# Experts' lists with entries of 64 B, written whole, in a kernel of decayed attention and a mixture of experts

## The chip, the core and the metric

The kernel runs on one core of a Trainium2 chip. The core has five engines with instruction streams of their own: TensorE (PE in the profile; its weight loads stand apart as PEld), VectorE (DVE), ScalarE (ACT), GpSimd (POOL) and SyncE (SP), which here only issues transfers. All transfers run on 16 DMA engines that the queues share: SP's and ACT's own queues, and a software queue that POOL issues on and that serves the indirect transfers, which scatter or gather rows by a list of indices. The metric is the device time of one execution in microseconds.

## The reference

```python
# attention with decay, per batch and head: 8 x 8 x 576 x 64
scores = (q @ k.T) / sqrt(64)
ret = scores * Dmat            # gamma_h ** (i - j) for i >= j, else 0
attn = ret @ v
# the rows of all heads side by side: x is 4608 x 512
logits = x @ w_gate            # 512 x 8
e_idx = argmax(logits, axis=1) # one expert of 8 for each token
gate_w = softmax(logits)[e_idx]
eom = sigmoid(x @ w_output_gate)
for e in range(8):
    mask = e_idx == e
    out[mask] = gate_w * eom[:, e] * (relu(x[mask] @ w1[e]) @ w2[e])
```

w1 is 8 x 512 x 1024, w2 is 8 x 1024 x 512; everything is float32. The scale of a row, `gate_w * eom`, is worked out as one reciprocal.

## The kernel before

**Retention part.** The 4608 tokens are 36 tiles of 128 rows, and a loop over `g` does one tile a step. SP loads the tile's q, k and v (`pk`, 768 KB in two transfers, five buffers, issued five steps ahead behind products of PE). POOL scales q (`prep_q`, `qs`, two steps ahead) and v (`prep_v`, `vs`, one step ahead). PE forms score products (`scores`), the result (`out_x`) and the running state (`update`), and transposes k (`k_rows`); DVE masks the scores and transposes the result, SP stores it to `xs` in DRAM (256 KB a step); ACT copies it to `xT` (line 413).

**Gate.** For each group of four tiles (`n`, nine groups) PE forms the logits, and the steps `gate_a`, `ranks`, `gate_b`, `exp_a`, `exp_b`, `gate_d` and `gate_c` give for each token its expert, its slot in that expert's list and its scale. The list `lst` lies in DRAM: eight lists of 4608 entries. An entry is two words, the token's number and its scale. `meta` holds both in SBUF, a pair of words for each of the 36 tiles; the numbers come from `tokid` by one load, `gate_c` writes the scales. Each tile's 128 entries go to `lst` by one indirect transfer of POOL (`scatter`, line 517, behind a memset of `tick`), queued in `todo` and issued one to two a step by `some`. Before the first scatter, `fill` writes all of `lst` with empty entries (token 4608, scale 0).

**Lists.** The main pass takes at most 616 tokens of an expert, as two parts of 360 and 256. `load_idx` reads the slots of these parts from `lst` to `lists` in SBUF on SP's queue, every 32 of them copied to all four quarters of the partitions, and `make_idx` turns them into indices on DVE: `idx` for whole rows, `gidx` for quarters of rows. This happens first for experts 0 and 1, part 0, behind step 30 (line 278, `make_idx` at step 32), and once more for everything else behind the last group's scatters. Each `load_idx` waits for every scatter so far. The rows themselves are gathered from `xs` by POOL (`gather_rows`, `gather`).

**Experts.** Each expert's products (`mm1`, `mm2`) split a float32 operand in a high and a low part and sum three products. The first three blocks of expert 0 run while the last group's gate is still being worked out; `transp_pe` of its part 1 (line 223, `t_ps`) is where PE needs the second list load. Tokens past 616 of an expert would be done by a loop at the end whose number of trips is read from `ovn`, a table that `overflow_table` makes at expert 1.

The order on each engine is the order in which the code is written; a scheduler doesn't move it.

Of the kernel before, what the change touches and what calls it, by code (L numbers as in the profile page):

```python
# [24 lines left out]
E = 8  # L25
# [17 lines left out]
SLOT = [[2 * (2 * (k % 2) + (c - k // 2) % 2) + k // 2 for c in range(2)] for k in range(4)]  # L43
NOV = 40


@with_exitstack
def tile_retention_moe(
# [28 lines left out]
    xs = dram.tile([NT + 1, DM], F32, name="xs")  # L77
    lst = dram.tile([E * NT, 2], I32, name="lst")

# [27 lines left out]
    def load_rest(step):  # L107
        if step == 1:
            SP.dma_start(out=wg_sb, in_=wg)
            SP.dma_start(out=csm_sb, in_=csm)  # L110
        if step == 2:
            SP.dma_start(out=cbf_sb, in_=cbf)
            SP.dma_start(out=meta, in_=tokid)

# [9 lines left out]

    NZ = E * NT // P // 3
    zw = xta.tile([P, KB * NW[0]], F32, name="xh0")[:, 0:512]
    zl = hpa.tile([P, NW[0]], I32, name="hh00")[:, 0:2 * NZ].rearrange("p (r w) -> p r w", w=2)
# [124 lines left out]
    def mm2(e, t, between={}):  # L252
# [3 lines left out]
        for fb in range(FB):  # L256
            wh, wl = (a[:, fb % 2, :] for a in W2[e, fb // 2])
            hh, hl = HT[e, part, fb]
            for a, b in ((hh, wh), (hh, wl), (hl, wh)):
                i = T.matmul(ps, lhsT=a[:, c0:c0 + n], rhs=b, start=(j == 0), stop=(j == 3 * FB - 1))  # L260
                j += 1
                if j in between:
# [4 lines left out]
                             in_=y, in_offset=None, bounds_check=NT - 1, oob_is_err=False)  # L267

    def load_idx(e0, e1, part):
        s0, t0, nb = part * NS[0], part * 4 * TA, NB[part]  # L270
        rest = NS[part] - 32 * nb
        view = lst.rearrange("(e a s) w -> e a s w", e=E, a=1)
        dmas = []
        if e1 - e0 < 4:

            for e in range(e0, e1):
                v = view[e, :, s0:s0 + 32 * nb].rearrange("a (j t) w -> a j (t w)", t=nb).broadcast_to([4, 32, 2 * nb])
                dmas.append(SP.dma_start(out=lists[:, e, t0:t0 + nb].rearrange("p t w -> p (t w)"), in_=v))
# [12 lines left out]
    def make_idx(e0, e1, part):  # L291
        n, t0 = (TA, 0) if part == 0 else (CT - TA, TA)
        V.tensor_scalar(out=gidx[:, e0:e1, 4 * t0:4 * (t0 + n)], in0=lists[:, e0:e1, 4 * t0:4 * (t0 + n), 0],
                        scalar1=4.0, scalar2=quad, op0=ALU.mult, op1=ALU.add)
        for a in range(4):
            q = slice(32 * a, 32 * a + 32)
            V.tensor_copy(idx[q, e0:e1, t0:t0 + n],
                          lists[q, e0:e1].rearrange("j e (t u) w -> j e t u w", u=4)[:, :, t0:t0 + n, a])

# [207 lines left out]
    def gate_c(n):  # L507
        zs, sli = gt["zs"], gt["sli"]
        es = sm.tile([P, GT, 1], F32, name="es")
        V.tensor_reduce(out=es, in_=gt["ex"], op=ALU.add, axis=AX.X)  # L510
        V.tensor_scalar(out=zs, in0=zs, scalar1=1.0, scalar2=None, op0=ALU.add)
        V.scalar_tensor_tensor(out=zs, in0=es, scalar=1e-9, in1=zs, op0=ALU.add, op1=ALU.mult)
        V.reciprocal(out=meta.bitcast(F32)[:, n * GT:(n + 1) * GT, 1:2], in_=zs)  # L513

        def scatter(t, dep=None):
            G.memset(tick, 0.0)
            i = G.indirect_dma_start(out=lst, out_offset=bass.IndirectOffsetOnAxis(ap=sli[:, t, :], axis=0),  # L517
                                     in_=meta[:, n * GT + t, :], in_offset=None)
# [19 lines left out]
    V.memset(zl[:, :, 0:1], NT)  # L538
    V.memset(lists, 0)
    V.memset(lists[:, :, :, 0:1], NT)  # L540
    factors(1)
# [7 lines left out]
    for g in range(NTILE):  # L549
# [183 lines left out]
    with ExitStack() as octx:  # L733
# [43 lines left out]
def _consts():  # L777
# [20 lines left out]
    tok = np.arange(NT).reshape(NG, GT, 4, 32).transpose(1, 3, 0, 2).reshape(P, NTILE)  # L798
    tok = np.stack([tok, 0 * tok], axis=2)
    f = np.float32  # L800
# [47 lines left out]
```

## Time and profile before

| | |
|---|---|
| runs | 609.34 us median of 3 (606.75 to 609.36) |
| profiled execution | 610.28 us, of which the span of its instructions 608.5 us |
| mean granted clock of TensorE | 0.984 |
| busy, share of the span: PE, PEld, DVE, ACT, POOL | 577.9 us 95%, 511.3 us 84%, 328.9 us 54%, 170.0 us 28%, 317.0 us 52% |
| DMA | 93.30 MB, 153 GB/s on the mean; 40.6% of the engines' time for SP's queue, 10.4% for POOL's |
| scatters to `lst` | 36, from 40.3 us to 179.0 us |

A row of a view gives a line of the code, the engine, the operation, what it writes and reads, how often, and its time; what stands in square brackets or behind the last bar is the time that the engine was idle before it, and what ended that. "issue" is a wait that the profile cannot name. In the rows of slices, each place is a stretch of time and each digit the busy share in tenths; a busy share of PE takes in time in which a product is waiting in the pipeline.

### The profile page before, as it was taken

The numbers are of one execution on the slowest core, as the hardware profiler recorded it, in microseconds if no ns is written. First come the engines' busy times: TensorE is split into PE (matmuls) and PEld (weight loads), VectorE is DVE, ScalarE is ACT, GpSimd is POOL, SyncE is SP. The second block draws the span as 40 slices with busy tenths as digits, with TensorE's granted clock in tenths as the row PEclk, the third lists the DMA queues.
The fourth block names the chain that finished last, engine by engine and source line by source line (L and its number), as shares of the span: only waits on it lengthen the run. The fifth ranks groups of instructions, "written<-read, shape, count | busy, mean of one in ns | idle before, by whom it ended". The sixth has DMA issues, their size and how long they took to land. (4 is left out here: it accounts for less than half of the span.)

```text
span 608.5 us, 14048 instructions
## 1 busy us (share of the span) xinstructions
PE 577.9 (95%) x5737; PEld 511.3 (84%) x5737; DVE 328.9 (54%) x640; ACT 170.0 (28%) x360; POOL 317.0 (52%) x333
## 2 busy tenths in 40 slices
PE   7989798888899999999999999999999999999995
PEld 4878687777797989979988997998899799879974
DVE  3567577576772769735841862484187239426300
ACT  5434233223542322132222221222222222212210
POOL 4778588675766754464453545345345534540011
PEclk9999899888999999999999999999999999999999
DMA  8899999877965546422721552263155216321001
GB/s 325 270 321 245 201 253 260 229 215 191 248 152 123 169 162 196 143 74 88 233 95 50 180 172 71 78 209 107 65 157 165 97 48 225 118 67 52 1 36 44
DMA packets 52420, 93.30 MB, mean 153 GB/s; under 512 B 10878, under 2 KB 30335, under 8 KB 52354
## 3 DMA queue, kind: packets, MB, share of 16 engines
q1 hardware_dynamic: 42690, 71.87, 40.6%
q0 software_dynamic: 9232, 19.93, 10.4%
q8 instruction: 46, 0.75, 0.5%
q10 hardware_dynamic: 432, 0.59, 0.3%
q14 instruction: 20, 0.16, 0.1%
HBM read 73.19 MB, written 19.86 MB: 153 GB/s over the span
## 5 line engine op out<-in xcount | busy, mean ns | idle before, releaser
L180 POOL DMA_INDIRECT x_q<-xs,gidx x140 | 148.0, 1057 | 108.6 <-ACT hh L248 71.0
L244 PE MATMUL h_ps<-xh,w1l 128*128 128x360 f32 (+1 forms) x512 | 154.6, 302 | 0.0
L244 PE MATMUL h_ps<-xh,w1h 128*128 128x360 f32 (+1 forms) x512 | 154.6, 302 | 0.0
L244 PE MATMUL h_ps<-xl,w1h 128*128 128x360 f32 (+1 forms) x512 | 154.5, 302 | 0.0
L260 PE MATMUL y_ps<-w2h,hh 128*128 128x512 f32 (+1 forms) x320 | 125.1, 391 | 0.3 <-ACT hh L248 0.3
L260 PE MATMUL y_ps<-w2l,hh 128*128 128x512 f32 (+1 forms) x320 | 124.8, 390 | 0.0
L260 PE MATMUL y_ps<-w2h,hl 128*128 128x512 f32 (+1 forms) x320 | 124.7, 390 | 0.0
L266 POOL DMA_INDIRECT out_dram<-y,idx x40 | 40.8, 1020 | 120.8 <-ACT y L265 105.7
L244 PEld LDWEIGHTS h_ps<-xh,w1l 128*128 128x128 f32 x512 | 96.9, 189 | 0.2 <-issue 0.2
L244 PEld LDWEIGHTS h_ps<-xl,w1h 128*128 128x128 f32 x512 | 96.2, 188 | 0.5
L244 PEld LDWEIGHTS h_ps<-xh,w1h 128*128 128x128 f32 x512 | 96.1, 188 | 0.5 <-issue 0.2
L248 ACT ACTIVATE hh<-h_ps 128x360 fp32r<-128x360 f32 (+1 forms) x128 | 54.6, 429 | 144.8 <-PE h_ps L244 143.8
L249 DVE SCALAR_TENSOR_TENSOR hl<-h_ps,hh 128x360 fp32r<-128x360 f32 (+1 forms) x128 | 58.5, 473 | 67.7 <-ACT hh L248 67.6
L260 PEld LDWEIGHTS y_ps<-w2h,hl 128*128 128x128 f32 (+1 forms) x320 | 58.8, 184 | 14.4 <-DVE hl L249 0.4
L260 PEld LDWEIGHTS y_ps<-w2h,hh 128*128 128x128 f32 (+1 forms) x320 | 58.8, 184 | 14.2 <-ACT hh L248 0.7
L260 PEld LDWEIGHTS y_ps<-w2l,hh 128*128 128x128 f32 (+1 forms) x320 | 58.7, 184 | 13.5
L265 ACT ACTIVATE y<-y_ps,idx 128x512 f32<-128x512 f32 (+1 forms) x40 | 27.5, 688 | 130.1 <-issue 68.9
L374 DVE TENSOR_TENSOR S_sb<-sc,cmat_sb 128x512 f32<-128x512 f32 x72 | 46.1, 681 | 29.6 <-PE sc L370 29.4
L336 POOL TENSOR_TENSOR qs<-pk,gq_sb 128x512 f32<-128x512 f32 x36 | 46.0, 1277 | 23.8 <-DMA pk<-in_pack_dram 9.0
L217 DVE TENSOR_TENSOR xl<-x_t,xh 128x512 fp32r<-128x512 f32 (+1 forms) x35 | 23.5, 673 | 64.0 <-ACT xh L214 64.0
L370 PEld LDWEIGHTS sc<-qs,pk 64*64 64x64 f32 x1152 | 28.6, 138 | 20.5 <-issue 14.2
L517 POOL DMA_INDIRECT lst<-meta,sli x36 | 37.6, 1043 | 14.2 <-DVE meta L513 9.0
(120 smaller groups left out, 623.5 us busy)
## 6 DMA issues: line engine op xcount, KB each, us to landing
st<-in_w_dram SPq DMA_DIRECT2D x61, 512.0 KB
pk<-in_pack_dram SPq DMA_DIRECT2D x31, 512.0 KB
pk<-in_pack_dram SPq DMA_DIRECT2D x32, 256.0 KB
xs<-xq SPq DMA_DIRECT2D x40, 128.0 KB
pk<-in_pack_dram SPq DMA_DIRECT2D x4, 768.0 KB
x_q<-xs,gidx POOLq DMA_INDIRECT x140, 3.9
xs<-w2h SPq DMA_DIRECT2D x16, 128.0 KB
xs<-w2l SPq DMA_DIRECT2D x16, 128.0 KB
```

The lines of the kernel that those rows point to most:

```text
L180: after(G.indirect_dma_start(out=XG[e, t][:, u, :], out_offset=None, in_=xs.rearrange("t (a c) -> (t a) c", a=4), in_offset=bass.IndirectO ...
L217: V.tensor_tensor(out=lo, in0=src[:, :, 0:n], in1=hi.bitcast(F32), op=ALU.subtract)
L244: T.matmul(ps, lhsT=a[:, k, :], rhs=b[:, k, :], start=(j == 0), stop=(j == 3 * KB - 1))
L248: done = A.activation(out=hh, in_=ps, func=AF.Relu)
L249: V.scalar_tensor_tensor(out=hl, in0=ps, scalar=0.0, in1=hh.bitcast(F32), op0=ALU.max, op1=ALU.subtract)
L260: i = T.matmul(ps, lhsT=a[:, c0:c0 + n], rhs=b, start=(j == 0), stop=(j == 3 * FB - 1))
L265: A.activation(out=y, in_=ps, func=AF.Copy, scale=idx.bitcast(F32)[0:n, e, t, 1:2])
L266: G.indirect_dma_start(out=out, out_offset=bass.IndirectOffsetOnAxis(ap=idx[0:n, e, t, 0:1], axis=0), in_=y, in_offset=None, bounds_check= ...
L336: G.tensor_tensor(out=qs[g], in0=pk[g][:, 0].rearrange("p (n i) -> p n i", n=NP), in1=gq_sb[:, c % 5], op=ALU.mult)
L370: last = T.matmul(sc[r][64 * h:64 * h + 64, p, i], lhsT=pk[g][s, 1, P * p + 64 * h:P * p + 64 * h + 64], rhs=qs[g][s, p, i], start=True, s ...
L374: V.tensor_tensor(out=S_sb[:, r].rearrange("p (a b) i -> p a b i", a=2), in0=sc[r].rearrange("p (a b) i -> p a b i", a=2), in1=m, op=ALU.mult)
L517: i = G.indirect_dma_start(out=lst, out_offset=bass.IndirectOffsetOnAxis(ap=sli[:, t, :], axis=0), in_=meta[:, n * GT + t, :], in_offset=None)
```

## The change

An entry of `lst` becomes 16 words (64 B) of which the first two are used. `meta` becomes two buffers of one group each, cleared at the start, so that a scatter writes whole entries; the token numbers stay in `toks` and a copy on DVE puts a group's into its buffer behind the reciprocal. `lists` is two tiles now: `lists0` for the first load, and one in the memory that the retention part has left, allocated and cleared behind the third block of `mm1`. Only the column of slots that a load fills in part is made empty beforehand (`empty`). `fill` covers 640 slots of each list in two transfers. The overflow loop, when it runs, first writes an empty block behind an expert's last token, whose place comes from six more operations in `overflow_table`. `gate_d`, with the copy of the slots to `sli`, is called ahead of `exp_b`.

```diff
+LW, LE = 16, 640
...
-    lst = dram.tile([E * NT, 2], I32, name="lst")
+    lst = dram.tile([E * NT + P, LW], I32, name="lst")
...
-    meta = const.tile([P, NTILE, 2], I32, name="meta")
-    lists = const.tile([P, E, CT * 4, 2], I32, name="lists")
+    toks = const.tile([P, NTILE, 1], I32, name="toks")
+    meta = [const.tile([P, GT, LW], I32, name=f"meta{i}") for i in range(2)]
+    lists0 = const.tile([P, 2, TA * 4, LW], I32, name="lists0")
...
-        for i in range(3):
-            SP.dma_start(out=lst.rearrange("(i p r) w -> i p r w", p=P, i=3)[i], in_=zl)
+        rows = lst[0:E * NT, :].rearrange("(e s) w -> e s w", e=E)[:, 0:LE].rearrange("e (p i r) w -> i e p (r w)", i=2, r=NZ)
+        for i in range(2):
+            SP.dma_start(out=rows[i], in_=zl.rearrange("p r w -> p (r w)"))
...
-                v = view[e, :, s0:s0 + 32 * nb].rearrange("a (j t) w -> a j (t w)", t=nb).broadcast_to([4, 32, 2 * nb])
+                v = view[e, :, s0:s0 + 32 * nb].rearrange("a (j t) w -> a j (t w)", t=nb).broadcast_to([4, 32, LW * nb])
...
+    def empty(lists):
+
+        V.memset(lists[:, :, NB[0]:NB[0] + 1, :], 0)
+        V.memset(lists[:, :, NB[0]:NB[0] + 1, 0:1], NT)
...
-        V.reciprocal(out=meta.bitcast(F32)[:, n * GT:(n + 1) * GT, 1:2], in_=zs)
+        m = meta[n % 2]
+        V.reciprocal(out=m.bitcast(F32)[:, :, 1:2], in_=zs)
+        V.tensor_copy(m[:, :, 0:1], toks[:, n * GT:(n + 1) * GT])
...
-                                     in_=meta[:, n * GT + t, :], in_offset=None)
+                                     in_=m[:, t, :], in_offset=None)
...
         elif n >= 0 and late == 2:
+            gate_d(n)
             exp_b(n)
-            gate_d(n)
...
+    lists1.append(pools["y"].tile([P, E, CT * 4, LW], I32, name="lists", bufs=1))
+    empty(lists1[0])
...
+            ie = ov.tile([P, 2], I32, name="ie")
+            V.memset(ie, 0)
+            V.memset(ie[:, 0:1], NT)
+            SP.dma_start(out=lst[bass.ds(z, P), 0:2], in_=ie)
```

Where it moves instructions or waits, at three places; in square brackets stands what a row waits for, engines by name, DMA queues' semaphores by number (DMASW for POOL's queue, DMAHW for SP's). The first is DVE in the gate of the first group, ahead of and behind `sli`, before and then after:

```order
L422 STREAM_TRANSPOSE w2l_660<-o_ps 128x4x4x32 [waits Activation_49]
L497 CAST sli<-lg_ps 128x4 [waits Activation_49]
L374 TENSOR_TENSOR S_sb<-sc_129,cmat_sb 128x512 [waits PE_49]
L374 TENSOR_TENSOR S_sb<-sc_130,cmat_sb 128x512 [waits PE_49]
L422 STREAM_TRANSPOSE w2l_660<-o_ps 128x4x4x32 [waits Activation_49]
L510 TENSOR_REDUCE es<-ex 128x4
L511 TENSOR_SCALAR lg_ps<-lg_ps 128x4 [waits DVE_49]
L512 SCALAR_TENSOR_TENSOR lg_ps<-es,lg_ps 128x4 [waits DVE_49]
L513 RECIPROCAL meta<-lg_ps 128x4 [waits DMAHW3_49,DVE_49]
```

```order
L437 STREAM_TRANSPOSE w2l_663<-o_ps 128x4x4x32 [waits Activation_49]
L512 CAST sli<-lg_ps 128x4 [waits DVE_49]
L389 TENSOR_TENSOR S_sb<-sc_131,cmat_sb 128x512 [waits PE_49]
L389 TENSOR_TENSOR S_sb<-sc_132,cmat_sb 128x512 [waits PE_49]
L437 STREAM_TRANSPOSE w2l_663<-o_ps 128x4x4x32 [waits Activation_49]
L525 TENSOR_REDUCE es<-ex 128x4
L526 TENSOR_SCALAR lg_ps<-lg_ps 128x4 [waits DVE_49]
L527 SCALAR_TENSOR_TENSOR lg_ps<-es,lg_ps 128x4 [waits DVE_49]
L529 RECIPROCAL meta_87<-lg_ps 128x4 [waits DVE_49]
L530 COPY meta_87<-toks 128x4 [waits DMAHW3_49]
```

The cast keeps its place on DVE and waits for DVE's own slots in place of ACT's exponential; a copy of the token numbers stands behind the reciprocal.

The second is DVE at the end of the last group's gate, between the blocks of `mm1` for expert 0 (`hl` is the low part of a hidden block, `w1l` that of a weight), before and then after:

```order
L513 RECIPROCAL meta<-lg_ps 128x4 [waits DVE_49]
L249 SCALAR_TENSOR_TENSOR hl_2980<-h_ps,hh_2979 128x360 [waits Activation_49]
L159 TENSOR_TENSOR w1l_3004<-st,w1h_2875 128x1024 [waits DMAHW3_49]
L249 SCALAR_TENSOR_TENSOR hl_3048<-h_ps,hh_3047 128x360 [waits Activation_49]
L249 SCALAR_TENSOR_TENSOR hl_3065<-h_ps,hh_3064 128x360 [waits Activation_49]
```

```order
L529 RECIPROCAL meta_87<-lg_ps 128x4 [waits DVE_49]
L530 COPY meta_87<-toks 128x4
L255 SCALAR_TENSOR_TENSOR hl_2992<-h_ps,hh_2991 128x360 [waits Activation_49]
L165 TENSOR_TENSOR w1l_3016<-st,w1h_2886 128x1024 [waits DMAHW2_49]
L312 MEMSET lists 128x8x16 [waits Pool_49]
L313 MEMSET lists 128x8 [waits DVE_49]
L255 SCALAR_TENSOR_TENSOR hl_3063<-h_ps,hh_3062 128x360 [waits Activation_49]
```

The two memsets of the second list tile stand between a weight's low part and the next `hl`, with a wait for POOL.

The third is SP's queue at the second list load, before and then after:

```order
L148 DMA st<-in_w_dram 128x1024 [waits DMAHW7_49,DVE_49,Activation_49]
L278 DMA lists<-lst 128x1x16 [waits DMASW5_49,DMASW4_49,DMASW6_49,DMASW3_49,DMASW7_49,DMASW2_49,DMAHW0_49,DMASW1_49,DMASW0_49]
L278 DMA lists<-lst 128x1x16 [waits DMAHW1_49]
L282 DMA lists<-lst 32x6x22 [waits DMAHW2_49]
L286 DMA lists<-lst 8x6x2 [waits DMAHW3_49]
```

```order
L154 DMA st<-in_w_dram 128x1024 [waits DMAHW6_49,DVE_49,Activation_49]
L287 DMA lists<-lst 128x1x128 [waits DMASW4_49,DMASW5_49,DMASW3_49,DMASW6_49,DMASW2_49,DMASW7_49,DMASW1_49,DMAHW7_49,DMASW0_49,Pool_49]
L287 DMA lists<-lst 128x1x128 [waits DMAHW0_49]
L291 DMA lists<-lst 32x6x176 [waits DMAHW1_49]
L295 DMA lists<-lst 8x6x16 [waits DMAHW2_49,DVE_49]
```

The transfers keep their places and their waits for all scatters, and each carries eight times the words.

More of the change, by code (lines that the diff above doesn't have):

```diff
@@ L44 @@
 NOV = 40
+COV = 2 * NOV + E * E + E
+PADC = 104
+LW, LE = 16, 640
 @with_exitstack
@@ L112, in load_rest @@
             SP.dma_start(out=cbf_sb, in_=cbf)
-            SP.dma_start(out=meta, in_=tokid)
+            SP.dma_start(out=toks[:, :, 0], in_=tokid)
     def factors(s):
@@ L122, in factors @@
                              scale=ratio[:, p, s - 1 + h:s + h])
-    NZ = E * NT // P // 3
+    NZ = LE * E // P // 2
     zw = xta.tile([P, KB * NW[0]], F32, name="xh0")[:, 0:512]
-    zl = hpa.tile([P, NW[0]], I32, name="hh00")[:, 0:2 * NZ].rearrange("p (r w) -> p r w", w=2)
+    zl = hpa.tile([P, NW[0]], I32, name="hh00")[:, 0:LW * NZ].rearrange("p (r w) -> p r w", w=LW)
     def fill():
-        for i in range(3):
-            SP.dma_start(out=lst.rearrange("(i p r) w -> i p r w", p=P, i=3)[i], in_=zl)
+        rows = lst[0:E * NT, :].rearrange("(e s) w -> e s w", e=E)[:, 0:LE].rearrange("e (p i r) w -> i e p (r w)", i=2, r=NZ)
+        for i in range(2):
+            SP.dma_start(out=rows[i], in_=zl.rearrange("p r w -> p (r w)"))
         SP.dma_start(out=xs[NT:NT + 1, :].rearrange("a (p r) -> (a p) r", p=P), in_=zw[:, 0:4])
@@ L267, in mm2 @@
                              in_=y, in_offset=None, bounds_check=NT - 1, oob_is_err=False)
+    lists1 = []
     def load_idx(e0, e1, part):
@@ L271, in load_idx @@
         rest = NS[part] - 32 * nb
-        view = lst.rearrange("(e a s) w -> e a s w", e=E, a=1)
+        lists = lists0 if (e0, part) == (0, 0) else lists1[0]
+        view = lst[0:E * NT, :].rearrange("(e a s) w -> e a s w", e=E, a=1)
         dmas = []
@@ L292, in make_idx @@
         n, t0 = (TA, 0) if part == 0 else (CT - TA, TA)
+        lists = lists0 if (e0, part) == (0, 0) else lists1[0]
         V.tensor_scalar(out=gidx[:, e0:e1, 4 * t0:4 * (t0 + n)], in0=lists[:, e0:e1, 4 * t0:4 * (t0 + n), 0],
@@ L297, in make_idx @@
             V.tensor_copy(idx[q, e0:e1, t0:t0 + n],
-                          lists[q, e0:e1].rearrange("j e (t u) w -> j e t u w", u=4)[:, :, t0:t0 + n, a])
+                          lists[q, e0:e1].rearrange("j e (t u) w -> j e t u w", u=4)[:, :, t0:t0 + n, a, 0:2])
+    def empty(lists):
+        V.memset(lists[:, :, NB[0]:NB[0] + 1, :], 0)
+        V.memset(lists[:, :, NB[0]:NB[0] + 1, 0:1], NT)
     actx = ExitStack()
@@ L538, in tile_retention_moe @@
     V.memset(zl[:, :, 0:1], NT)
-    V.memset(lists, 0)
-    V.memset(lists[:, :, :, 0:1], NT)
+    empty(lists0)
+    for m in meta:
+        V.memset(m, 0)
     factors(1)
@@ L639, in tile_retention_moe @@
     pools["ht1"] = mctx.enter_context(tc.tile_pool(name="hpb", bufs=1, side="right", reuse_waits="tile"))
-    ovt = const.tile([1, 2, NOV], I32, name="ovt")
+    ovt = const.tile([1, 3, NOV], I32, name="ovt")
     ovn = const.tile([1, 1], I32, name="ovn")
@@ L646, in overflow_table @@
         T.matmul(n_ps, lhsT=cbf_sb[:, 1, :], rhs=cum, start=True, stop=True)
-        cov_sb = pools["y"].tile([1, 2 * NOV + E * E + 112], F32, name="cov", bufs=1)[:, 0:2 * NOV + E * E]
+        cov_sb = pools["y"].tile([1, COV + PADC], F32, name="cov", bufs=1)[:, 0:COV]
         SP.dma_start(out=cov_sb, in_=cov)
@@ L738, in tile_retention_moe @@
             e = nc.values_load(ovt[0:1, 0, bass.ds(i, 1)], engines=[mybir.EngineType.SP], min_val=0, max_val=E - 1)
-            o = nc.values_load(ovt[0:1, 1, bass.ds(i, 1)], engines=[mybir.EngineType.SP], min_val=0,
-                               max_val=E * NT - P)
+            o, z = (nc.values_load(ovt[0:1, r, bass.ds(i, 1)], engines=[mybir.EngineType.SP], min_val=0,
+                                   max_val=E * NT) for r in (1, 2))
+            ie = ov.tile([P, 2], I32, name="ie")
+            V.memset(ie, 0)
+            V.memset(ie[:, 0:1], NT)
+            SP.dma_start(out=lst[bass.ds(z, P), 0:2], in_=ie)
             io = ov.tile([P, 2], I32, name="io")
-            SP.dma_start(out=io, in_=lst[bass.ds(o, P), :])
+            SP.dma_start(out=io, in_=lst[bass.ds(o, P), 0:2])
             wa = ov.tile([P, KB, F], F32, name="wa")
@@ L809, in _consts @@
         "cov": np.concatenate([np.arange(NOV), np.arange(NOV) * P,
-                               np.tril(np.ones((E, E))).reshape(-1)])[None].astype(f),
+                               np.tril(np.ones((E, E))).reshape(-1), np.arange(E)])[None].astype(f),
     }
```

11 lines of the change are left out of this document (9 added, 2 removed).

## The prediction

> **What bounds the kernel now.** I read the page first, for the slices of PE and DMA, then the windows by stage, then single waits.
>
> ```profile
> PE   7989798888899999999999999999999999999995
> DMA  8899999877965546422721552263155216321001
> ```
>
> One slice is 15.2 us. PE is full from the twelfth slice on (the experts' matrix products); only in the first eleven, the retention part, does it fall to 7 and 8, and there the DMA engines stand at 8 and 9.
>
> The next fence is the view of windows: length, busy time of each engine, granted clock, DMA share, GB/s. The one behind it shows the copy of each 128-row tile's result to xT on ACT, once per step of the loop over g; I cut the windows at these copies (steps 8, 16, 20, 31 and 35).
>
> ```profile
> core 0: us, PE busy (x) PEld busy (x) DVE busy (x) ACT busy (x) POOL busy (x), PEclk, DMA share, GB/s
> 12.70:41.21 28.51, 27.51 (x706) 23.92 (x701) 19.28 (x44) 13.57 (x35) 20.35 (x19) 1.00 0.94 300
> 41.21:79.69 38.48, 32.48 (x722) 27.81 (x724) 22.01 (x60) 12.16 (x29) 27.84 (x34) 0.91 0.93 231
> 79.69:93.96 14.27, 13.44 (x345) 11.65 (x341) 11.00 (x30) 5.19 (x13) 12.66 (x17) 1.00 0.99 277
> 93.96:144.71 50.75, 44.42 (x1020) 37.98 (x1014) 33.54 (x86) 16.45 (x39) 37.58 (x45) 0.93 0.88 226
> 144.71:165.13 20.42, 16.26 (x332) 13.70 (x331) 13.75 (x41) 9.77 (x19) 13.30 (x17) 0.92 0.89 232
> 165.13:200.00 34.87, 33.94 (x210) 29.89 (x211) 18.76 (x43) 11.74 (x20) 22.56 (x27) 1.00 0.65 153
> 200.00:608.50 408.50, 401.61 (x2333) 361.38 (x2331) 206.95 (x330) 95.75 (x193) 177.62 (x171) 1.00 0.35 113
> ```
>
> ```profile
> 41.21 0.59 ACT L413 COPY xT<-o_ps 128x512 f32<-128x512 f32 x1 [1.87 <-PE o_ps L405]
> 79.69 0.59 ACT L413 COPY xT<-o_ps 128x512 f32<-128x512 f32 x1 [1.66 <-PE o_ps L405]
> 93.96 0.59 ACT L413 COPY xT<-o_ps 128x512 f32<-128x512 f32 x1 [1.66 <-PE o_ps L405]
> 144.71 0.59 ACT L413 COPY xT<-o_ps 128x512 f32<-128x512 f32 x1 [1.97 <-PE st_ps L387]
> 165.13 0.59 ACT L413 COPY xT<-o_ps 128x512 f32<-128x512 f32 x1 [1.13 <-PE o_ps L405]
> ```
>
> From step 8 to 31 there are 23 steps in 103.50 us, 4.50 us each. In the good stretch in the middle, 79.69 to 93.96, four steps (a whole group with its gate, ranks and scatters) take 14.27 us: 3.57 each, at clock 1.00. Step 8 is where the scatters to the list begin. Before it, DMA moved 300 GB/s, behind it 231 and 226 at nearly the same busy share: the engines are occupied, but by packets that do not move on.
>
> What holds them I read where little else runs: four scatters in a row, last on POOL, and then the load of the lists, which waits for them on SP. DMA and GB/s rows are of the window 175 to 190, 0.375 us a place.
>
> ```profile
> 175.18 0.96 POOL L517 DMA_INDIRECT lst<-meta,sli  x1 [4.13 <-DVE meta L513]
> 178.97 1.12 POOL L517 DMA_INDIRECT lst<-meta,sli  x1 [0.19 <-issue]
> DMA  9798674310000000000099002090000500531513
> GB/s 153 208 328 252 220 219 197 121 14 0 0 3 0 0 0 3 0 0 0 0 66 76 0 11 22 0 175 0 0 0 0 153 22 0 131 64 13 53 4 45
> 186.62 1.15 SPq L278 DMA_DIRECT2D lists<-lst  x2
> SPq L278 <- DMA lst<-meta,sli: 13.1, 2, 10.7
> ```
>
> The last scatter is issued by 180.09 and its packets show by 181 (the 3 at the sixteenth place); the engines then stand empty, yet SP is released only at 186.6, after 10.7 us of waiting. So 1 KB in 128 pieces of 8 B needs some 6 us behind the last packet before it counts as landed. Four scatters are 512 pieces; from the first issue they took 11.4 us, or about 20 ns a piece one after the other (estimate from these rows), 2.6 us a scatter.
>
> Under load the same shows as holes. Scatter at 111.03, then DMA from 112 to 119 in places of 0.175 us:
>
> ```profile
> 111.03 1.01 POOL L517 DMA_INDIRECT lst<-meta,sli  x1 [0.20 <-issue]
> DMA  0000079948899842994931346799989999969999
> GB/s 0 0 0 4 2 164 257 117 47 47 47 211 70 47 47 23 94 70 70 140 23 47 94 140 257 316 398 410 398 331 386 372 445 326 347 214 334 385 407 430
> q0 software_dynamic: 60, 0.00, 0.6%
> ```
>
> Behind the scatter's packets (places 4 and 5) the load of a tile crawls at 23 to 140 GB/s with busy engines for some 3 us, then runs at 400. The scatters' own packets (q0) take 0.6% of the engines: it is not their bytes, it is what they do to everybody else's. Rows of 2 KB scattered through the same software queue do not behave so; the last number is the median from issue to landing:
>
> ```profile
> lst<-meta,sli POOLq DMA_INDIRECT x36, 5.9
> out_dram<-y,idx POOLq DMA_INDIRECT x40, 2.8
> ```
>
> How that reaches PE:
>
> ```profile
> 59.52 0.90 PE L370 MATMUL sc<-qs,pk 64*64 64x128 f32 x32
> 70.90 0.37 PE L348 MATMUL kt<-ident,pk 128*128 128x128 f32 x1 [2.84 <-issue]
> 71.20 1.56 PE L370 MATMUL sc<-qs,pk 64*64 64x128 f32 x32
> 147.55 0.60 PE L370 MATMUL sc<-qs,pk 64*64 64x64 f32 x18 [2.18 <-issue]
> ```
>
> PE stops for 2.84 us amid four like transposes, for nothing the profile names ("issue"), while DMA is in such a hole; the 32 score products then take 1.56 us in place of 0.90, at a lowered clock. I read the stop as instructions arriving late by DMA, which no row proves.
>
> **The change, part by part.** *Entries of 64 B.* 36 scatters keep 128 rows each; each row becomes a whole entry of 16 words where it was 2 words that shared neighbouring bytes. That adds 36 x 128 x 56 B = 258 KB, 0.7 us of DMA over the stage at 380 GB/s (the end of the GB/s row above). The price of a row of 64 B is in no row here. Its bounds are the 8 B scatter (5.9 us to landing, holes of about 3 us) and the 2 KB scatter (2.8 us, none). I take the end of the 2 KB rows: both write bytes that no other row shares, and the 8 B pieces are slow one after the other, as writes that share a unit of memory would be. Then the holes go, and the next limit is POOL's own chain:
>
> ```profile
> 82.46 1.28 POOL L336 TENSOR_TENSOR qs<-pk,gq_sb 128x512 f32<-128x512 f32 x1
> 83.69 1.05 POOL L341 TENSOR_TENSOR vs<-pk,gk_sb 128x512 f32<-128x512 f32 x1
> 84.67 0.11 POOL L516 MEMSET tick<- 128x1 f32 x1
> 84.94 1.01 POOL L517 DMA_INDIRECT lst<-meta,sli  x1 [0.16 <-issue]
> 85.98 1.28 POOL L336 TENSOR_TENSOR qs<-pk,gq_sb 128x512 f32<-128x512 f32 x1
> ```
>
> 3.52 us from one qs to the next without a pause, which the change leaves as it is. A step moves 1 MiB (three quarters of it pk, one quarter xs), 2.8 us at 380 GB/s, so DMA is under POOL then. I take the 3.57 of the good stretch as the pace: 23 x (4.50 - 3.57) = **21.4 us**. For the last four steps (20.42 us, clock 0.92), 14.3 at that pace plus the twelve transposes and the gathers' landing, some 18: **2.4 us**.
>
> *The end of the list.* The chain that leads from the last scatter to PE:
>
> ```profile
> 189.48 0.23 DVE L293 TENSOR_SCALAR gidx<-lists,csm_sb 128x16 int32<-128x16 int32 x1 [4.29 <-DMA lists<-lst]
> 194.32 0.63 PE L223 MATMUL t_ps<-ident,x_q 128*128 128x128 f32 x4 [0.93 <-DMA x_q<-xs,idx]
> ```
>
> With a landing of 3 us behind the last issue, the lists load at about 183, 3.6 us sooner, and PE's 0.93 us go: **0.9 us**. Against it, each list load carries eight times the bytes: the second batch 8 x (16 + 66 + 48) KB = 1.04 MB, 2.8 us at 380 GB/s, ahead of the gather that PE waits for. Only the first two loads (128 KB) are ahead of gidx; the rest has the 3.6 us as its cover. Were that gone, the 2.8 us would fall on PE.
>
> *DVE.* Nine copies of token numbers into the entries:
>
> ```profile
> L497 DVE CAST sli<-lg_ps 128x4 int32<-128x4 f32 x9 | 1.4, 157 | 5.0 <-ACT lg_ps L505 4.2 <-ACT kn L353 0.7
> L674 DVE TENSOR_REDUCE cs<-ge 1x40 f32<-1x320 f32 x1 | 0.5, 474 | 0.0
> ```
>
> At 157 ns like the cast, 1.4 us over nine groups; in the good stretch DVE is busy 11.00 of 14.27 us, which covers 0.16 per four steps. The moved gate copy no longer waits for ACT (the row's 4.2 us, in 3 waits): DVE idle time in front of a score mask that waits for PE anyway, so nothing. Six more operations in the overflow table are at most 6 x 0.47 = 2.8 us (the second row is the like of the longer ones) at expert 1, beside PE's products, where DVE is busy half the time; zero. The second clearing of lists stands between a weight split and a hl; two short memsets that wait for a POOL operation of the retention part, long done; zero, or about 2 x 0.47 us if hl's cover, five PSUM banks, were gone. Start-up memsets: as many and as large as before, under the first loads. Fill: 320 KB for 288. The overflow loop has no trip in this trace, since no row of its lines shows, and its added DMA costs nothing.
>
> Sum: 21.4 + 2.4 + 0.9 = 24.7. Against the profiled execution, 610.28 us (span 608.5 plus 1.8 around it), that is 585.6; the median of the runs, 609.34, stands 0.9 lower. Forecast **585 us**.
>
> **Rivals.**
> [...]
> 2. *Only part goes.* If the holes halve, or PE's stops come from something else than scatters, the pace falls to about 4.1: 23 x 0.4 + 0.9 = 10, so 600 (593 to 603). For it: PE's stop of 2.18 us ahead of 147.55, behind the first list load, which waits until all scatters have landed.
> 3. *Slower: the list loads.* If the scatters still land 6 us late, 1.04 MB lies in front of x_q's gather: 2.8 us at 380 GB/s, 4.7 at 226. PE waits 0.9 + 2.8 to 4.7, and the time is 612 to 615. It decides where landing gains less than 2.8 us.
>
> **How the numbers follow.** The forecast's own range is 578 to 593. At 3.45 us, POOL's four operations end to end, in all 27 steps, the gain would be 23 x 1.05 + 4 x 1.65 + 0.9 = 32; at 3.85, with the last four steps 1 us shorter, 23 x 0.65 + 1 + 0.9 = 17. I give it 0.65, rival 2 0.18, rival 1 0.12, rival 3 0.05. 577 to 603 takes in the forecast and rival 2, 0.83. What a measurement can tell from no change is about 0.5%, 3 us: faster 0.83, same 0.11 (rival 1 mostly), slower 0.06.
>
> **What would show it.** The median landing of lst at about 3 us; no holes at high busy share behind scatters; the windows between steps 8 and 35 at clock 1.00 and above 280 GB/s; steps of 3.4 to 3.8 us with POOL nearly without idle time; SP's wait for lst under 5 us and no wait of PE for x_q; the stretch from the first h_ps product on unchanged in length. It is wrong if the landing stays near 6 us, or if it falls and the steps still take over 4 us: then PE's "issue" stops had another source.

## The result and the profile after

The changed kernel takes **600.31 us** (median of 4, 598.89 to 600.49), the kernel before, on the same chip, 609.35 (606.75 to 609.65): a ratio of 0.9856, 95% interval 0.9825 to 0.9887. That is 9.0 us of the 24.7 that the sum had: inside the wide range (577 to 603), outside the forecast's own (578 to 593), and at the 600 us of rival 2. On another chip (e12 in the experiments, 6 runs), the ratio was 0.9789 (0.9744 to 0.9834). The medians of the kernel before differ by chip: 609 to 611 us on three of them, 619 and (one run) 620 on the other two, so totals are compared as ratios on one chip, and stages from the profiles.

The slices of PE, its clock and the DMA engines; one slice is 15.0 us now:

```profile
PE   7998999797999999999999999999999999999995
PEclk8999999999899999999999999999999999999998
DMA  8898899879546446225521732362164216321001
```

The retention part fills PE better, and its last step (35) is reached at 154.96 us in place of 165.13. The windows, cut at the same steps' copies to xT (steps 0, 8, 31 and 35), of the kernel after; behind it the stretch of before from step 8 to 31 in one piece, which the prediction showed in three, and a part of it:

```profile
12.67:42.37 29.70, 28.76 (x706) 24.96 (x703) 19.24 (x45) 13.78 (x35) 19.94 (x19) 0.96 0.94 296
42.37:133.08 90.71, 82.68 (x2059) 71.04 (x2061) 65.76 (x182) 33.90 (x80) 77.91 (x94) 1.00 0.89 273
133.08:154.96 21.88, 17.59 (x350) 14.36 (x344) 14.13 (x44) 10.12 (x20) 13.99 (x18) 0.85 0.71 215
```

```profile
41.21:144.71 103.50, 90.35 (x2071) 77.44 (x2071) 66.55 (x176) 33.80 (x79) 78.08 (x94) 0.93 0.91 235
70.40:77.00 6.60, 6.10 (x85) 5.35 (x84) 2.27 (x6) 1.61 (x4) 2.19 (x3) 0.50 0.87 230
```

| stretch | before, us | after, us | difference | forecast |
|---|---|---|---|---|
| start to step 8 | 41.21 | 42.37 | +1.2 | 0 |
| step 8 to 31 | 103.50 | 90.71 | -12.8 | -21.4 |
| step 31 to 35 | 20.42 | 21.88 | +1.5 | -2.4 |
| step 35 to the end | 443.37 | 443.74 | +0.4 | -0.9 |

The 12.8 us have two parts. PE's busy time fell by 7.7 us (90.35 to 82.68) though it does the same products: the clock was 0.93 on the mean and is 1.00. Before, it stood at half in three stretches, of which the second row shows the longest: 0.50 for 6.6 us, right behind the stop of 2.84 us that the prediction quotes. The other 5.1 us are PE's idle time, 13.15 us before (103.50 - 90.35) and 8.03 after.

A scatter in the middle, and DMA from 83 to 90 us, 0.175 us a place, as the prediction showed it for before:

```profile
83.26 1.01 POOL L534 DMA_INDIRECT lst<-meta,sli  x1 [0.16 <-issue]
DMA  8999889999396888979889899999985999969996
GB/s 331 410 337 304 281 278 302 386 258 202 114 202 190 187 164 263 304 301 337 313 328 363 319 360 328 357 307 278 293 237 202 298 304 272 310 260 293 316 334 208
```

Behind this scatter, the hole of 3 us at 23 to 140 GB/s has become a dip of about 1.2 us (seven places) at 114 to 258. Median landing of scatters and gathers (a trace holds the landing of at most five of the scatters to the list, so their medians rest on those), and the waits that the prediction named:

```profile
lst<-meta,sli POOLq DMA_INDIRECT x36, 4.1
pk<-xs,idx POOLq DMA_INDIRECT x3, 6.6
```

```profile
PE sc L229 <- DMA pk<-xs,idx: 3.9, 2, 2.3
PE sc L385 <- issue: 1.3, 1, 1.3
PE o_ps L420 <- issue: 0.7, 1, 0.7
PE st_ps L402 <- issue: 0.5, 1, 0.5
PE lg_ps L448 <- issue: 0.4, 1, 0.4
PE t_ps L229 <- DMA x_q<-xs,idx: 0.2, 1, 0.2
SPq L287 <- DMA lst<-meta,sli: 7.9, 3, 5.3
```

PE's stops for "issue" fell from 9.9 us to 2.9. The rows of before:

```profile
PE sc L370 <- issue: 4.7, 3, 2.2
PE kt L348 <- issue: 2.8, 1, 2.8
PE o_ps L401 <- issue: 1.3, 3, 0.6
PE st_ps L387 <- issue: 1.1, 2, 0.6
```

What grew is the first row of the changed kernel: PE waits 3.9 us for the rows that the gathers bring at steps 34 and 35, 1.6 us before.

### The profile page after: what moved, and what is told of

Its sections match the earlier page's. It is cut to its first block, busy times and chain, and to the rows that moved or that the text cites. A ratio compares the mean times of both kernels' runs of the same rounds, so it can differ in the third digit from the quotient of the medians.

```text
span 598.7 us, 14066 instructions
## 1 busy us (share of the span) xinstructions
PE 572.9 (96%) x5737; PEld 506.4 (85%) x5737; DVE 330.3 (55%) x659; ACT 170.6 (28%) x360; POOL 315.3 (53%) x333
## 5 line engine op out<-in xcount | busy, mean ns | idle before, releaser
L234 DVE STREAM_TRANSPOSE x_t<-x_q 128x512 f32<-128x512 f32 x35 | 24.7, 705 | 32.1 <-DMA x_q<-xs,gidx 32.1
```

Of the source, the lines that this page charges most:

```text
L234: V.transpose(out=src.rearrange("p k (u j) -> p u k j", u=4), in_=XG[e, t].rearrange("p u (k i) -> p u k i", k=KB))
```

## The experiments

For each run the table gives steps 8 to 31, PE's clock there, and the ratio to before on the same chip where the whole kernel was computed. In the diffs, `...` stands for what is left out.

| run | scatters | steps 8 to 31, us | clock | ratio, 95% |
|---|---|---|---|---|
| before; again | 8 B, packed | 103.50; 101.40 | 0.93; 0.97 | 1 |
| e1 | 8 B, packed | 100.99 | 0.95 | 0.9995 (0.9956 to 1.0033) |
| e10 | 16 B | 92.56 | 0.98 | 0.9864 (0.9812 to 0.9917) |
| e2 | 32 B | 89.36 | 1.00 | 0.9781 (0.9736 to 0.9827) |
| e3 | 8 B in 64 | 90.70 | 0.98 | 0.9804 (0.974 to 0.9869) |
| after; again (e12) | 64 B | 90.71; 88.40 | 1.00; 1.00 | 0.9856; 0.9789 |
| e4 | rows of 512 B | 88.96 | 1.00 | |
| e11 | 8 B, spread | 94.92 | 1.00 | |
| e5 | none | 88.11 | 1.00 | |
| e6 | none, POOL's time kept | 88.12 | 1.00 | |
| e7 | 64 B | 93.35 | 1.00 | 0.9838 (0.9792 to 0.9884) |
| e9 | 32 B | 90.31 | 1.00 | 0.9757 (0.9718 to 0.9796) |

Each stage time is one profile's. In after, e12 and e7 the code of these steps is the same, and they took 88.40 to 93.35 us; no run here explains the difference, so one of that size between two rows decides little by itself. Before, e8 and e1, with packed entries of 8 B, took 100.99 to 103.50.

### What makes a small scatter dear

**e1**: `LW = 2`, the rest as changed.

```diff
-LW, LE = 16, 640
+LW, LE = 2, 640
```

> The changed kernel with entries of 8 B again (2 words, packed), everything else of the change kept. Sharing theory (T: what costs is that pieces of several tokens lie in one 64 B unit of memory): the entry size is the whole change, so 606 to 610 us, landing of the scatters 5.5 to 6 us, half-clock episodes of PE back in steps 8 to 31. Rival O (the moved gate copy, the smaller clearing and the fill bring a part): 601 to 605.

**e2** (`LW = 8`) and **e10** (`LW = 4`) differ from it in that number alone.

> The changed kernel with entries of 32 B, written whole, two to a 64 B unit. T with a unit of 64 B: 604 to 609 us and a landing above 5 us, since neighbours still share. If 32 B is the unit, or if it is only the count of pieces per unit that matters and two are few: 599 to 602 us and a landing near 4.1 us. [...]

> The changed kernel with entries of 16 B, written whole: four to a 64 B unit, two to 32 B. If nobody may share 32 B (8 B slow, 32 B free): steps 8 to 31 about 96 to 100 us and landing between 4.5 and 6. If the number of pieces in a unit of 64 B decides and four are few enough: 89 to 91 us, landing 4.1 to 4.6. If any sharing costs as much as eight pieces do: 100 to 103 us.

**e3**: entries 64 B apart, 8 B written.

```diff
-            i = G.indirect_dma_start(out=lst, ...
-                                     in_=m[:, t, :], in_offset=None)
+            i = G.indirect_dma_start(out=lst.rearrange("s (h w) -> (s h) w", w=2), ...
+                                     in_=m[:, t, 0:2], in_offset=None)
...
-        V.tensor_copy(sli, slf)
+        V.tensor_scalar(out=sli, in0=slf, scalar1=8.0, scalar2=None, op0=ALU.mult)
```

> The changed kernel with entries 64 B apart of which a scatter writes only the first 8 B. T: nobody shares a unit, so 599 to 602 us and a landing near 4.1 us, as with whole entries. [...]

**e4**: rows of 512 B to a tensor of their own.

```diff
-            i = G.indirect_dma_start(out=lst, ...
-                                     in_=m[:, t, :], in_offset=None)
+            i = G.indirect_dma_start(out=far, ...
+                                     in_=ident, in_offset=None)
```

> The changed kernel with its 36 scatters writing rows of 512 B (the identity matrix's) to a tensor of their own, at the same slots; the lists stay empty, so routing and the experts' rows are left out and only the retention part is compared. T: 64 B whole is already free of sharing, so steps 8 to 31 stay at 3.85 to 4.0 us and landing at 3.5 to 4.2 us. [...]

The windows of steps 8 to 31 of e1, e10, e2, e3 and e4:

```profile
43.59:144.58 100.99, 87.83 (x2059) 75.45 (x2061) 66.23 (x181) 34.04 (x79) 77.77 (x94) 0.95 0.92 237
```

```profile
40.93:133.49 92.56, 84.67 (x2059) 72.84 (x2061) 66.15 (x182) 33.98 (x80) 78.04 (x94) 0.98 0.93 260
```

```profile
42.83:132.19 89.36, 82.81 (x2059) 71.20 (x2061) 65.87 (x182) 34.01 (x80) 77.92 (x94) 1.00 0.90 278
```

```profile
42.56:133.26 90.70, 84.26 (x2059) 72.74 (x2061) 65.70 (x181) 34.08 (x79) 77.76 (x94) 0.98 0.89 271
```

```profile
42.58:131.54 88.96, 81.87 (x2059) 70.88 (x2061) 65.79 (x181) 33.90 (x79) 77.90 (x93) 1.00 0.93 293
```

e1 is the kernel before in time and in its marks (GB/s 237, half clock, stops for issue); its landing, 7.1 us, is longer than the 5.5 to 6 expected. So the entry size is the change's whole effect, and all that the prediction costed at zero, which e1 keeps, is zero within 0.4% (2.4 us). Rival O falls. e3 writes the same 8 B as e1 and is as quick as whole entries (90.70 us; 88.40 to 93.35 for 64 B): neither that a piece is short nor that it fills only 8 of its 64 B is what costs (the trace holds none of e3's landings). e2, two entries to 64 B, shows that 64 B are not needed (89.36 us): theory T with a unit of 64 B expected 604 to 609 us there, the median was 597.79, and it falls; that there is a unit, and of what size, no run shows. e10, at 16 B, lies between its first two cases in time (92.56) and above both in landing (7.3 us); whether it keeps some of the loss is not shown, since its steps lie within the spread of 64 B and its ratio's interval overlaps that of e12 on the same chip. Rows of 512 B (88.96 us, landing 4.8) bring nothing over 64 B.

**e11** takes the kernel before, 8 B packed, and turns the slots' bits round, so that the pieces of one scatter don't meet in the same 64 B (neighbours there are 64 slots apart, which an expert fills in about one group of 512 tokens).

```diff
         V.tensor_copy(sli, slf)
+        V.tensor_scalar(out=lo, in0=sli, scalar1=63, scalar2=3, op0=ALU.bitwise_and, op1=ALU.logical_shift_left)
+        V.tensor_scalar(out=hi, in0=sli, scalar1=6, scalar2=7, op0=ALU.logical_shift_right, op1=ALU.bitwise_and)
+        V.tensor_tensor(out=lo, in0=lo, in1=hi, op=ALU.bitwise_or)
+        V.tensor_scalar(out=sli, in0=sli, scalar1=9, scalar2=9, op0=ALU.logical_shift_right, op1=ALU.logical_shift_left)
+        V.tensor_tensor(out=sli, in0=sli, in1=lo, op=ALU.bitwise_or)
```

> The kernel before with its packed entries of 8 B, but with the slots' bits turned round within each 512 entries, so that consecutive slots lie 64 B apart and a unit's eight entries are written by scatters that lie several groups apart. Five small operations on DVE per group are added; the lists then hold the tokens in another order with some left out, so only the retention part is compared. Theory T1 (pieces cost when they come to one unit at the same time): landing about 4 us, steps 8 to 31 at 89 to 93 us, as with 64 B entries. Rival T2 (a unit written in part, with others' bytes beside it, costs whenever that is): landing near 6 us and 100 to 104 us, as before.

Its window of steps 8 to 31, PE's largest wait and the landing:

```profile
43.52:138.44 94.92, 84.10 (x2059) 71.94 (x2061) 75.31 (x200) 33.80 (x79) 77.79 (x94) 1.00 0.85 256
...
PE sc L370 <- DVE S_sb L374: 5.8, 4, 2.2
...
lst<-meta,sli POOLq DMA_INDIRECT x36, 4.5
```

94.92 is above what T1 expected and well below T2. Most of the excess is put down to the trial itself: DVE does some 24 operations more (200 for 176 in before), and PE waits for DVE's score masks 5.8 us in four stops, where e1 has one of 1.3 us; without that difference it would be 90.4 (an estimate). Landing is 4.5 us, the clock 1.00 throughout. So packed pieces cost when those of one scatter lie side by side (100.99 to 103.50 us); the same packed list, written in another order, is nearly free.

### What the floor of a step is

**e5** has no scatters; **e6** has a product of POOL in the place of each.

```diff
-            i = G.indirect_dma_start(out=lst, ...
+            G.tensor_tensor(out=wst.tile([P, 512], F32, name="st"), in0=gq_sb[:, 0]..., in1=gq_sb[:, 0]..., op=ALU.mult)
```

> The changed kernel without its 36 scatters (the one-column memset ahead of each stays); the lists stay empty, so routing and the experts' rows are left out and only the retention part is compared. Theory P (what is left of the 3.9 us a step is the order of POOL's and PE's own work): POOL has 2.3 us a step in place of 3.5, so PE with its 3.35 us is the bound: steps 8 to 31 take 77 to 81 us in place of 90.7. Rival L (the loads of pk, tied to PE's progress, bound the step): 86 to 91 us, with or without scatters.

> As the run without scatters, but with a product of 128x512 on POOL (1.04 us, as long as a scatter's issue) in each scatter's place; the lists stay empty, so routing and the experts' rows are left out. P: POOL's time alone sets the step, so steps 8 to 31 take 88 to 91 us, as with scatters of 64 or 512 B, and step for step the same durations. Rival D (what is left comes from the scatters' packets among the loads): 77 to 82 us, as without scatters.

Steps 8 to 31 of e5, of e6, and of the changed kernel again (e12):

```profile
42.55:130.66 88.11, 82.39 (x2059) 71.03 (x2061) 64.45 (x183) 34.02 (x80) 53.86 (x69) 1.00 0.90 277
```

```profile
42.81:130.93 88.12, 82.78 (x2059) 71.39 (x2061) 67.70 (x181) 33.99 (x80) 76.92 (x93) 1.00 0.91 278
```

```profile
42.37:130.77 88.40, 82.34 (x2059) 70.94 (x2061) 65.69 (x181) 33.90 (x80) 77.67 (x94) 1.00 0.92 280
```

With POOL 53.86 us busy or 76.92, with scatters or without: 88 us. Theory P falls, since POOL's time doesn't bound these steps, and so does rival D. By these two profiles, scatters that cost nothing would leave 88 us for the 23 steps, 15.4 us under before. Why the "good stretch" was shorter is seen in e5, where nothing disturbs: an ordinary group of four steps, and the same four as in the prediction's stretch (steps 16 to 20):

```profile
57.52:72.78 15.26, 14.63 (x381) 12.77 (x377) 10.89 (x31) 6.36 (x15) 9.42 (x13) 1.00 0.88 273
72.78:87.05 14.27, 13.44 (x345) 11.64 (x341) 10.89 (x31) 5.28 (x12) 9.38 (x13) 1.00 0.97 296
```

The second holds the border between two pairs of batch rows (a pair fills nine tiles; g = 17 is the last of one, 18 the first of the next), where the state is neither updated nor used: 345 products for 381, and 1 us less. It took 14.27 us in before, and 14.27 without any scatters.

The 88 us lie in the range of rival L, the loads. Two runs on e5's base, without scatters, took work from one side each. **e13**:

```diff
-        made = out_x(g, S_sb, prev, lambda last: load(g + 5, 1, last) if g + 5 < NTILE else None)
+        made = out_x(g, S_sb, prev, lambda last: None)
...
-        G.tensor_tensor(out=vs[g], in0=pk[g][:, 2]...
+        G.tensor_tensor(out=vs[g], in0=pk[g][:, 2 if g < 5 else 0]...
```

> The run without scatters, and from step 5 on also without the loads of v (256 of the 768 KB of a step; POOL scales q's rows in v's place, so the attention's result is another one). Theory F (PE's own work, busy 82.4 of 88.1 us, is the floor): steps 8 to 31 stay at 87 to 88.5 us. Rival L (the loads bound the step): they fall to 75 to 83 us.

**e14**:

```diff
-            k_rows(g + 1)
+            if (g + 1) % CPB % 4 == 0:
+                k_rows(g + 1)
+            else:
+                kn[g + 1] = kn[g] if g in kn else kn[g - 1]
```

> The run without scatters, and with PE's four transposes of k and their copy left out in 15 of the 21 steps between 8 and 31 that have them (an older step's k stands in, so the state is another one). F: 15 x 0.57 to 0.66 us go from PE, and steps 8 to 31 fall by 7 to 10 us, to 78 to 81. Rival L: they stay above 86 us.

Steps 8 to 31 of e13 and of e14, and PE's waits there in e14:

```profile
42.90:128.67 85.77, 81.44 (x2059) 70.59 (x2061) 63.67 (x181) 34.06 (x80) 53.93 (x69) 1.00 0.75 214
```

```profile
43.97:129.26 85.29, 75.90 (x2002) 65.94 (x2004) 63.47 (x181) 25.56 (x64) 54.13 (x69) 1.00 0.93 286
...
PE sc L385 <- issue: 2.1, 3, 1.0
PE o_ps L416 <- DVE lg_ps L526: 1.6, 5, 0.4
PE o_ps L416 <- DVE sli L512: 1.5, 4, 0.5
```

Neither came out as F or L had it. A third of the bytes of the loads gone saves 2.3 us, and what is left is PE's 81.44 us and some 4 of waits, so loads are a part of the floor and not the whole. With 6.5 us of products gone, 2.8 us are saved: PE's idle time rises from 5.7 us (88.11 - 82.39) to 9.4, for DVE in the gate's steps and for "issue". So PE, busy 82.39 of 88.11 us, is the nearest to a bound, and DVE's steps and the loads stand close behind it; F was right on the engine and wrong on how far one can go. Both savings are of single profiles and smaller than the spread noted above.

### The half clock, and the last four steps

**e7** keeps PE busy where it waits.

```diff
+        for i in range({1: 9, 2: 7}.get(t, 0)):
+            T.matmul(banks[2][:, i % 4, :], lhsT=ident, rhs=ident, start=True, stop=True, skip_group_check=True)
...
+        if g == 0:
+            for i in range(3):
+                T.matmul(banks[2].rearrange("p a b -> p (a b)"), lhsT=zw[:, 0:P], rhs=zw, start=True, stop=True, ...
```

> The changed kernel with extra products on PE, into a bank that nobody needs then, where it waits: three of 128x512 at step 0 ahead of the second score products, nine and seven of 128x128 ahead of the transposes of the second and third gathered block at steps 34 and 35. Theory C (the half clock follows from PE's stops, and is what the first and the last steps lost): no half-clock stretch at 12 to 16 and 148 to 155 us, steps 0 to 8 about 28.5 us in place of 29.7, steps 31 to 35 about 19.5 in place of 21.9, so 595 to 598 us in all. Rival W (the half clock is covered by the waits for DMA): the clock reads 1.00 and the time stays at 599 to 601.

Steps 31 to 35 of e7; the changed kernel's stand above (21.88 us at 0.85):

```profile
136.09:157.68 21.59, 20.36 (x381) 17.14 (x376) 13.29 (x39) 9.85 (x20) 12.98 (x17) 1.00 0.71 218
```

The clock reads 1.00 from the first step to the last, where the changed kernel's read 0.96 in the first stage and 0.85 in the last, which supports that the half clock follows from PE's stops. But the steps are hardly shorter: steps 31 to 35 took 21.59 us and 0 to 8 took 30.27 (before, on that chip, 23.80 and 30.98; the changed kernel was not profiled there). Steps 8 to 31, where nothing was added, took 93.35 us, the longest of the three profiles of that code. The ratio to before (0.9838, 0.9792 to 0.9884) lies between the changed kernel's on its two chips. So C's gain did not come, and rival W has the total: the gathers' rows arrive no sooner for a quicker PE. That such a stretch costs its full price in steps 8 to 31, where PE waits least, is argued and not tried.

**e8** is the kernel before once more, on e7's chip.

> The kernel before, once more, for a second profile of it. C: the stretches of half clock come behind other stops or at other places than in the first profile, while the scatters land in the same 5.5 to 6.5 us; the time stays within 606 to 612. Rival: the stretches sit at the same steps, as part of the program's order.

Two of its stretches of half clock:

```profile
65.40:68.40 3.00, 3.00 (x36) 2.55 (x36) 1.68 (x6) 0.99 (x3) 2.04 (x3) 0.52 0.97 103
110.10:113.60 3.50, 3.50 (x61) 3.05 (x62) 1.22 (x5) 1.55 (x3) 1.82 (x3) 0.54 0.95 268
```

They lie at steps 12 and 22; in the first profile they lay at steps 14, 22, 27 and 31. So their places are partly the program's and partly an execution's. Its 623 us are above what was expected, and so are the 619 of before's other runs on that chip.

**e9** issues the three gathers at once, with entries of 32 B; **e12** is the changed kernel on the same chip.

```diff
-        if 32 <= g < 35:
-            gather_rows(g - 32)
+        if g == 32:
+            for t in range(TA):
+                gather_rows(t)
```

> The changed kernel with entries of 32 B and with the three gathers of rows for the first block issued one behind the other at step 32, where they were at steps 32, 33 and 34. Theory G (steps 31 to 35 are bound by the second and third gather's landing some 6 us behind an issue that comes late on POOL): both land 2 to 3 us sooner, PE's waits for them fall from 3.9 to about 1 us and the half clock there goes: steps 31 to 35 take 17.5 to 19 us in place of 21.9, and the whole is 3 to 5 us below the changed kernel on the same chip. Rival Q (qs and vs, pushed back by 2.1 us on POOL, now hold PE; or the gathers land as late beside the loads of weights): no change within 1.5 us.

> The changed kernel once more, on the chip of these runs: the reference for the run with the gathers at once, and a second profile. Steps 8 to 31 again within 1 us of 90.7, while steps 0 to 8 and 31 to 35 may move by 1 to 2 us from one execution to another, as the two profiles of the kernel before do (28.5 and 31.0; 20.4 and 23.8).

The gathers on POOL and PE's wait, steps 31 to 35 in e9; behind it the same gathers in the changed kernel's first profile:

```profile
137.27 1.06 POOL L199 DMA_INDIRECT pk<-xs,idx  x1 [4.57 <-DMA xl<-in_w_dram]
138.63 1.01 POOL L199 DMA_INDIRECT pk<-xs,idx  x1 [0.30 <-issue]
139.95 1.00 POOL L199 DMA_INDIRECT pk<-xs,idx  x1 [0.30 <-issue]
...
PE sc L229 <- DMA pk<-xs,idx: 0.2, 1, 0.2
...
131.09:149.06 17.97, 15.74 (x349) 13.04 (x343) 12.69 (x38) 9.92 (x20) 11.80 (x16) 1.00 0.81 235
```

```profile
138.13 1.06 POOL L199 DMA_INDIRECT pk<-xs,idx  x1 [3.44 <-DMA xs<-w2h]
141.65 1.05 POOL L199 DMA_INDIRECT pk<-xs,idx  x1 [0.16 <-issue]
143.94 1.04 POOL L199 DMA_INDIRECT pk<-xs,idx  x1 [0.16 <-issue]
```

The last gather leaves 2.7 us behind the first instead of 5.8, PE's wait and the half clock are gone, and steps 31 to 35 take 17.97 us; e12 took 22.93. Theory G holds for the stage. The whole kernel took 595.44 us (median of 6, ratio 0.9757, 0.9718 to 0.9796) and e12 597.87 (0.9789, 0.9744 to 0.9834): quicker by 2.4 us, with intervals that overlap. It has the lowest ratio here and is quicker than before; 3 to 5 us below the changed kernel were expected, and that it beats it as a whole is not shown. Its steps 8 to 31 took 90.31 us where e12's took 88.40, which gives back part of what the last steps gained, and it differs from e12 in the entries (32 B) as well. e12's own steps 8 to 31 came out 2.3 us below the 90.7 that were expected within 1 us.

## Why the prediction was right or wrong

**The mechanism was right.** Small pieces packed side by side hold the other transfers up (235 GB/s in steps 8 to 31 before and 237 in e1, 273 after), the cost is all in the entries, and entries apart remove most of it (steps 8 to 31 took 100.99 us in e1, 89.36 in e2, 90.70 in e3, 94.92 in e11). Of the prediction's reason, "writes that share a unit of memory", e11 shows this much: pieces of one scatter that lie side by side are what costs, and the same packed list written in another order is nearly free (90.4 us by the estimate above). That memory has such a unit, or its size, no run shows. Longer pieces bring no more: 8 B alone in their 64 B took 90.70 us, rows of 512 B 88.96. Rival 1, which was most of the 0.11 on "same", did not come (ratio 0.9856).

**The step that failed is the size of the first term**, 23 x (4.50 - 3.57) = 21.4 us, which came to 12.8 (15.1 with e12's 88.40 us). "I take the 3.57 of the good stretch as the pace" took for undisturbed what was light: those four steps have 345 products, 86.3 a step, while the rows that the prediction quoted beside it had 722 in eight and 1020 in eleven, 90.3 and 92.7. Undisturbed, the mean of the 23 steps is 3.83 us (e5). And the next limit is not "POOL's own chain": a step with 1 us less on POOL takes as long (e5, e6), and in the changed kernel POOL is busy for 77.91 of the 90.71 us, not nearly without idle time. In its place stands PE's own work, 82.39 of e5's 88.11 us, with DVE and the loads close behind. From the floor of 88.1 the most that the term could have been is 15.4, and the change has taken five sixths of it or more.

**The clock** was in the quoted rows (0.91 and 0.93) and had no term of its own. PE's busy time fell by 7.7 of the 12.8 us as the half clock went; that all of it is the clock's is not shown, since busy time at 1.00 is 81.87 us in e4 and 84.68 in e7. One of the three stretches of half clock follows the "issue" stop of 2.84 us. The other two, from about 107.5 and 128 us on, follow waits for POOL and for DVE:

```profile
107.32 1.49 PE L405 MATMUL o_ps<-S_sb,vs 128*64 128x128 f32 x16 [2.21 <-POOL qs L336]
127.99 1.26 PE L370 MATMUL sc<-qs,pk 64*64 64x128 f32 x30 [1.51 <-DVE S_sb L374]
```

The last of these stops is still in the changed kernel (1.28 us, at 118.32), without a half clock behind it; e3 has it (1.27 us) with one. So a stop's length alone does not decide. At the start it doesn't either: of the 15 profiles of kernels that have a stop there (1.8 to 3.0 us long, ending at 10.2 to 10.8 us), 10 show a half clock (0.50) behind it, among them the one with the shortest stop (1.83 us, e1) and not the one with the longest (3.04 us, before). What decides no run here shows.

**"Issue" stops** as late instructions got some support, no proof. In the stop of before from 68.06 to 70.90 us lands one packet of the queue that the profile calls instruction (one row of the DMA queues from 68 to 69 us):

```profile
q8 instruction: 1, 0.02, 5.8%
```

With the holes gone, PE's issue stops fell from 9.9 to 2.9 us. The prediction would have been wrong in this reason if they had stayed.

**The last four steps** were to gain 2.4 us and lost 1.5. The term counted transposes and took the gathers' landing as if it would give way; it is 6.6 us (6.1 before), and PE's wait for it grew from 1.6 to 3.9 us; that PE arrives ahead of it because its steps come sooner is argued. The 18 us of the forecast are there once the gathers leave earlier (e9, 17.97). Between executions this stage moves, too: 20.42 and 23.80 in the two profiles of before, 21.88 and 22.93 in those of after, so the 1.5 us itself is within what the profiles differ by.

**The end of the list** did as forecast in its own waits: SP issues the second list load at 171.40 us, 1.3 us behind the end of the last scatter's issue (6.5 before), PE's wait for x_q went from 0.93 to 0.2 us, and rival 3 did not come. SP's wait for the lists, forecast under 5 us, is 7.9 in three waits, the longest 5.3. Yet step 35 to the end did not get 0.9 us shorter but 0.4 longer, by a term that the prediction put at zero, the six operations in the overflow table:

```profile
247.54 0.47 DVE L699 TENSOR_TENSOR ge<-eo,cov 1x320 f32<-1x320 f32 x1
249.68 0.71 DVE L234 STREAM_TRANSPOSE x_t<-x_q 128x512 f32<-128x512 f32 x1
251.68 0.47 PE L266 MATMUL y_ps<-w2h,hh 128*104 128x512 f32 x1 [1.37 <-ACT y L271]
```

The first of the six starts at 247.54; they hold a transpose back to 249.68, ACT's copy `xh` (250.42) waits for that, ACT's `y` (250.95) stands behind `xh`, and PE waits 1.37 us for `y`. Before, PE has no such wait. That DVE is busy half the time on the mean (55% of the span) did not cover 2.1 us in one piece.

**Landing** was forecast at 3 us and is 4.1 and 4.8 in the median, for rows of 512 B as well (4.8). The 2.8 us of the output's scatters, which the forecast took over, come from a stage in which the DMA engines are a third busy (0.35 from 200 us on). Nor is landing the measure of harm: e10's scatters land in 7.3 us, its steps take 4.02, and the two landings that before has in steps 8 to 31, 3.9 and 3.3 us, lie among the changed kernel's three (3.0, 6.2 and 3.0).

**The start** (+1.2 us) had no term, and needs none (though the memsets there are six and not four, "as many", of fewer words in all): step 8 was reached at 40.8 to 44.7 us in the profiles of kernels that differ little up to there.

**Rival 2** had the number, 600, but not by its reason: the holes did not halve into a pace of 4.1; they nearly went, and the pace underneath was slower than thought.

## What to carry to other kernels

Before you take a stretch as the pace without a disturbance, count its work: products, or bytes, per step, against the stretch that it is to stand for. Words of 8 B that a scatter put side by side were dear for the transfers beside it (235 GB/s in steps 8 to 31 before, 273 after), not in their own bytes (0.6% of the engines' time in the prediction's 7 us); give each 32 or 64 B of its own (89.36 us; 88.40 to 93.35), or an order in which the pieces of one scatter lie apart (94.92). A stop of PE of 1.3 to 2.8 us can cost more than itself where PE is the bound, since products at half clock may follow (behind the 2.84 us of before, 32 score products took 1.56 us in place of 0.90); where PE waits for a transfer anyway, those were nearly free (the last four steps took 21.59 us at 1.00 in e7, 21.88 at 0.85 in the changed kernel), and it helped that stage to let the transfer leave earlier (17.97 us in e9). Work that an engine has room for on the mean can still be paid for where it stands in one piece ahead of something that PE needs (2.1 us on DVE, a wait of 1.37 us on PE).

## What the runs showed of the hardware

- Scattered pieces of 8 B cost as much as rows of 512 B when no other piece of the same scatter lies within the same 64 B (90.70 and 88.96 us for 23 steps); packed side by side they cost 101 to 103.5. At 32 B, two to 64 B, nothing is left to see (89.36); 16 B (92.56) lie within the spread of the code with 64 B (88.40 to 93.35).
- With those packed pieces, two or three stretches at a clock of 0.50 lie in steps 8 to 31 in each of three profiles (before, e8, e1); with 32 B or more, none or one (e3). They follow stops of PE of 1.3 to 2.8 us, of which some wait for other engines, and last 3 to 6.6 us; a stop of 1.28 us was followed by none in the changed kernel.
- The landings that the traces have for scatters of 128 pieces beside other work overlap whatever the piece: 3.0 to 6.2 us for 64 B (after), 3.2 to 5.7 for 512 B (e4), 3.3 to 9.6 for packed 8 B (before). The GB/s of the whole stage tells the packed entries apart (234 to 237 in before, e8 and e1; 262 to 293 with 32 B or more and in e3), the landing doesn't.
